# Scores of both head groups in one run of PE tiles inside the batch loop of a fused attention and two-layer kernel

## The chip, the cores and the metric

The kernel runs on one core of one Trainium2 chip. The metric is the device time of one execution in microseconds (us); the time before is 1316.52 us, the median of three runs (1315.59 to 1317.91).

## What is computed

Batch is 8, heads 8, sequence 576, head size 64; `p` holds 32 packed queries per head. All arithmetic is float32.

```python
def sm_attn(qq, kk, vv):
    s = scale * np.matmul(qq, kk.transpose(0, 1, 3, 2))
    s = s - np.max(s, axis=-1, keepdims=True)
    a = np.exp(s)
    a = a / (np.sum(a, axis=-1, keepdims=True) + 1e-09)
    return np.matmul(a, vv)
p_packed = sm_attn(p, k, v)
out = sm_attn(q, p_packed, p_packed)
x = out.transpose(0, 2, 1, 3).reshape(B * S, H * D)      # 4608 x 512
h = np.maximum(np.maximum(x @ w1, x @ w2), x @ w3)       # 512 -> 768
x = h @ w_out                                            # 768 -> 512
h = x @ w_in                                             # 512 -> 2048
return (h * np.cos(h)) @ w_out2                          # 2048 -> 512
```

## The kernel before, in words

**Numbers.** Large products run in three passes on operands split into a rounded part (hi) and a remainder (lo). ACT copies the hi part, DVE or POOL subtracts to get the lo part. Scores, transposes and the small products of attention stay in plain f32.

**Units.** The eight heads of a batch form two head groups, g = 0 and 1, of four heads; `Unit(b, g)` (L413) holds one. Phase 1 of a unit turns p, k and v into the packed rows: `ld_k`, `ld_v` (loads), `S1` (scores of p against k, through `scores`, L451), `S1m` (row maximum, DVE), `E1` (exponential, ACT), `T1` (transposes), `PV1` (product with v and normalization), `BT` (one more transposition, into `bt`). Phase 2 makes the attention weights of the 576 queries: `ld_q`, `S2` (scores of q against `bt`), `S2t` (DVE transpose out of PSUM), `S2r` (maximum and subtraction), `X2a` (exponential), `X2b` (sum and normalization), `X2t` (transpose back), `X2c` (`ch`, `cl`: hi and lo parts). `scores` issues eight products of 64 rows by 32 columns of the PE array: two row halves (hh) by two heads (pi) make four of the array's eight 64x32 tiles, and two steps cover the 576 columns as 2x288. Each f32 product is two matmul instructions in the trace, so one unit's scores are 16 instructions.

**Folds.** The packed rows are multiplied into w1, w2, w3 beforehand. `fold(b, j, g)` (L677) makes piece j (0 to 4, four blocks of 128 columns each, the last half as wide) of group g for batches b and b+1 at once: eight products on all eight 64x32 tiles (`fold_p`, L637), then per half an ACT copy and a DVE subtraction out of PSUM into one of five `zx` buffers, then two DMAs (`fold_z`, L665): one into a z buffer (six of them) for the even batch, one to DRAM for the odd batch.

**Batches.** `gemm1_p` (L707) is one of 18 products h of a batch (12 matmuls each; product u uses fold piece u // 4); `gemm2_p` (L735) are eight half products x after them. A batch has 26 positions: 0 to 17 for h, 18 to 25 for x.

**Stages and their order.** (1) The first stage does the weight conversion and batches 0 and 1. Its order is worked out by a list planner (`Order`, L46) from assumed costs, with random nudges to its priorities given by the list `FIRST`. (2) The loop (L1359) does batches 2 to 5. At position p of batch b, `att_pos` (L853) issues the folds that `FOLDS` places there and the attention steps that `PLANS` places there, before the product of that position; phase 1 works for batch b+2, phase 2 for b+1. `conv_pos` (L820) does the same for pieces of the later weights: load, four passes over ACT, POOL and DVE, store to DRAM. There are NC2 = 18 of these pieces. (3) The last stage does batches 6 and 7, the remaining folds of batch 6, the conversion of the 14 weight pieces that the loop did not do (L1486 to L1508, POOL, ACT, DVE), and the first 16 chunks of the cosine layer (products L1281 and L1388); its order comes from the planner with the list `LAST`. (4) The rest of the cosine layer, in an order of its own (`Flow`).

**PSUM.** `big` (two banks, L421) is the one tile of the attention steps in the loop; `f` is two tiles of one bank each for the folds; `ps_m` holds two tiles for h and x. Every engine works its instructions in the order of issue, and all loads and stores here go through the queue of SP.

Of the kernel before, what the change touches and what calls it, by code (L numbers as in the profile page):

```python
# [29 lines left out]
)  # L30
LAST = (
# [213 lines left out]
def tile_pack_attention_max_moe_cos_moe(  # L245
# [35 lines left out]
    NZX, NCV, NZP, NC2, TS = 5, 6, 6, 18, 2  # L281
# [74 lines left out]
    with tc.manual_schedule():  # L356
# [6 lines left out]
        def small(ap):  # L363
            for _ in range(2):
                ap.tile([P, 4], F32, tag="st", bufs=2, name="st")
            ap.tile([P, 48], F32, tag="ms", name="ms")

        class Res:
            def __init__(self):
# [4 lines left out]
                small(ap)  # L374

        class Res32:
            def __init__(self, n, ps):
# [3 lines left out]
                small(self.ap)  # L381
# [11 lines left out]
        ps_f = mctx.enter_context(tc.tile_pool(name="ps_f", bufs=2, space=PSUM, reuse_waits="tile"))  # L393
# [19 lines left out]
        class Unit:  # L413
# [120 lines left out]
            def Pb(self):  # L534
                self.bd = self.res.ap.tile([P, D], F32, tag="pv", bufs=2, name="pv")
# [35 lines left out]
            def r2(self):  # L571
                ms = self.res.ap.tile([P, 48], F32, tag="ms", name="ms")
# [51 lines left out]

        def w_mov(j, kc):
# [24 lines left out]
        def fold_a(b, j, g, pi):  # L650
            ps = fx[b, j, g][pi]
            x = zx.tile([P, 2, UB * P], F32R, tag="w", name="zx")[:, :, :ps.shape[-1]]
            own = half_of(b, j, pi)
# [3 lines left out]
        def half_of(b, j, pi):  # L657
            return slice(D - pi * D, P - pi * D) if b == 0 and j in alone else slice(0, P)
# [1279 lines left out]
```

## Time and profile before

| What | Value |
|---|---|
| median of three runs | 1316.52 us |
| the profiled execution, its own time | 1318.48 us |
| span of its trace, first to last instruction | 1316.5 us |
| PE (TensorE matmuls) busy | 1274.5 us (97%) |
| DVE (VectorE) busy | 867.5 us (66%) |
| ACT (ScalarE) busy | 684.0 us (52%) |
| POOL (GpSimd) busy | 310.2 us (24%) |
| mean granted clock of TensorE | 0.987 of full speed |

The stages lie in the trace at 0 to 187 us (first), 187 to 449 (loop, some 64 us a batch), 449 to about 730 (last stage) and from there to the end. PE's busy share says that it seldom waits; what a change is worth is read from the waits of its own stage. The profiled execution is 2.0 us above the median of the runs.

### The profile page before, as it was taken

The numbers are of one execution on the slowest core, as the hardware profiler recorded it, in microseconds if no ns is written. First come the engines' busy times: TensorE is split into PE (matmuls) and PEld (weight loads), VectorE is DVE, ScalarE is ACT, GpSimd is POOL, SyncE is SP. The second block draws the span as 40 slices with busy tenths as digits, with TensorE's granted clock in tenths as the row PEclk, the third lists the DMA queues.
The fourth block names the chain that finished last, engine by engine and source line by source line (L and its number), as shares of the span: only waits on it lengthen the run. The fifth ranks groups of instructions, "written<-read, shape, count | busy, mean of one in ns | idle before, by whom it ended". The sixth has DMA issues, their size and how long they took to land.

```text
span 1316.5 us, 24190 instructions
## 1 busy us (share of the span) xinstructions
PE 1274.5 (97%) x9290; PEld 1105.9 (84%) x9290; DVE 867.5 (66%) x1438; ACT 684.0 (52%) x1318; POOL 310.2 (24%) x284
## 2 busy tenths in 40 slices
PE   6789999999999999999999999999999999999998
PEld 3468987988798799977888899999999999999897
DVE  6966455756566662698588696657666576666655
ACT  4543234333323332354455677666666666666665
POOL 4551003351424100261011023212132121321100
PEclk9789999999999999999999999999999999999999
DMA  9877469759975898446012555756557565575630
GB/s 338 290 218 225 141 176 282 275 219 286 288 272 205 247 285 298 177 131 246 33 64 98 182 192 192 237 191 228 185 170 253 186 233 183 170 252 189 219 132 32
DMA packets 111026, 270.54 MB, mean 206 GB/s; under 512 B 15680, under 2 KB 39232, under 8 KB 110912
## 3 DMA queue, kind: packets, MB, share of 16 engines
q1 hardware_dynamic: 110912, 269.01, 61.1%
q8 instruction: 73, 1.20, 0.4%
q14 instruction: 41, 0.34, 0.1%
HBM read 190.32 MB, written 61.87 MB: 192 GB/s over the span
## 4 chain that ended last, share of the span: by engine, by line
PE 87%; DMA 6%; DVE 4%; issue 1%; ACT 1%; SPq 0%; POOL 0%; DVEq 0%; ACTq 0%; POOLq 0%
PE po L1753 27%; PE g L1715 20%; PE h L714 16%; PE x L747 12%; PE g L1281 5%; PE zps L645 2%; PE po L1388 2%; PE big L458 2%; DMA z<-zx 2%; DMA raw<-kT 1%; DMA raw<-v 1%; PE big L526 1%; DMA zd<-zx 1%; DVE y L1308 1%; DMA wraw<-w_out 1%
## 5 line engine op out<-in xcount | busy, mean ns | idle before, releaser
L1753 PE MATMUL po<-w,gh 128*128 128x512 f32 x1560 | 367.5, 390 | 0.0
L1753 PEld LDWEIGHTS po<-w,gh 128*128 128x128 f32 x1560 | 288.1, 188 | 56.5
L1715 PEld LDWEIGHTS g<-xc,wr 128*128 128x128 f32 x2160 | 259.0, 188 | 5.6 <-DVE hs L1738 0.7
L1715 PE MATMUL g<-xc,wr 128*128 128x256 f32 x2160 | 261.8, 278 | 0.2
L714 PE MATMUL h<-at,z 128*128 128x256 f32 (+1 forms) x1728 | 251.5, 302 | 5.4 <-DMA z<-zx 4.6
L714 PEld LDWEIGHTS h<-at,z 128*128 128x128 f32 x1728 | 233.4, 192 | 27.6 <-issue 16.0
L1234 POOL TENSOR_TENSOR xc<-xr,xc 128x256 fp32r<-128x256 f32 x92 | 81.5, 904 | 494.3 <-ACT xc L1230 463.9
L747 PEld LDWEIGHTS x<-hh,w 128*128 128x128 f32 x1152 | 153.8, 190 | 11.8 <-issue 6.2
L747 PE MATMUL x<-hh,w 128*128 128x320 f32 (+1 forms) x1152 | 159.0, 297 | 1.7 <-DVE m L729 1.7
L1738 DVE TENSOR_TENSOR hs<-mc,g 128x256 f32<-128x256 f32 x168 | 70.4, 421 | 136.5 <-PE g L1715 130.0
L729 DVE TENSOR_TENSOR m<-m,h 128x576 f32<-128x576 f32 x96 | 72.2, 752 | 93.3 <-PE h L714 83.6
L1320 ACT ACTIVATE y<-y 128x512 f32<-128x512 f32 x144 | 91.0, 632 | 63.1 <-DVE y L1316 61.6
L1310 DVE SCALAR_TENSOR_TENSOR y<-y 128x512 f32<-128x512 f32 x128 | 96.6, 755 | 41.1 <-ACT y L1302 39.7
L1344 DVE TENSOR_TENSOR gh<-y,gh 128x512 fp32r<-128x512 f32 x144 | 107.8, 749 | 21.9 <-ACT gh L1340 21.0
L1726 ACT COPY mc<-g 128x256 f32<-128x256 f32 x168 | 62.2, 373 | 108.5 <-PE g L1715 108.3
L1340 ACT CAST gh<-y 128x512 fp32r<-128x512 f32 x144 | 89.6, 622 | 49.1 <-DVE y L1324 49.1
L1281 PE MATMUL g<-x,w 128*128 128x512 f32 x384 | 92.0, 389 | 0.0
L1281 PEld LDWEIGHTS g<-x,w 128*128 128x128 f32 x384 | 72.0, 188 | 14.9
L1302 ACT ACTIVATE y<-y 128x512 f32<-128x512 f32 x128 | 81.0, 633 | 4.1
L1324 DVE TENSOR_TENSOR y<-y,hs 128x512 f32<-128x512 f32 x112 | 80.9, 726 | 3.3 <-ACT y L1320 3.1
L1316 DVE TENSOR_SCALAR y<-y 128x512 f32<-128x512 f32 x144 | 78.4, 544 | 3.2
L663 DVE TENSOR_TENSOR zx<-zps,zx 128x512 fp32r<-128x512 f32 (+2 forms) x80 | 48.0, 631 | 36.5 <-ACT zx L654 35.0
(105 smaller groups left out, 1296.4 us busy)
## 6 DMA issues: line engine op xcount, KB each, us to landing
wr<-sd SPq DMA_DIRECT2D x152, 512.0 KB, 4.6
zd<-zx SPq DMA_DIRECT2D x64, 256.0 KB, 4.6
z<-zd SPq DMA_DIRECT2D x32, 512.0 KB, 5.9
z<-zx SPq DMA_DIRECT2D x56, 256.0 KB, 4.6
wr<-sd SPq DMA_DIRECT2D x56, 256.0 KB, 3.6
sd<-w SPq DMA_DIRECT2D x24, 512.0 KB, 4.9
wraw<-w_out SPq DMA_DIRECT2D x22, 512.0 KB, 6.1
wraw<-w SPq DMA_DIRECT2D x18, 512.0 KB, 5.9
```

The lines of the kernel that those rows point to most:

```text
L714: nc.tensor.matmul(ps[:, T0 + c0:T0 + c0 + nt], zt[b, j, g][:, x, c:c + P], at[b, g][:, y, c0:c0 + nt], start=(n == 0), stop=(n == 3 * NG ...
L747: nc.tensor.matmul(ps[:, T0 + c0:T0 + c0 + nt], w[:, x, d * P:(d + 1) * P], hh[f][:, y, c0:c0 + nt], start=(f == 0 and (x, y) == passes[0] ...
L1234: EITHER[eng].tensor_tensor(out=x[:, 1, kk, :], in0=x_part(t, *XSRC[i], kk), in1=x[:, 0, kk, :].bitcast(F32), op=ALU.subtract)
L1281: nc.tensor.matmul(ps, w[:, a, kc * P:(kc + 1) * P], x2[t, kc][:, b, :], start=(n == 0), stop=(n == 3 * KC - 1),)
L1302: nc.scalar.activation(out=r, in_=y, func=AF.Copy, scale=1.0, bias=MAGIC)
L1310: nc.vector.scalar_tensor_tensor(out=y, in0=r, scalar=MAGIC, in1=y, op0=ALU.subtract, op1=ALU.subtract)
L1320: nc.scalar.activation(out=r, in_=y, func=AF.Sin, scale=TWO_PI if c < NF2 else -TWO_PI)
L1324: nc.vector.tensor_tensor(out=r, in0=r, in1=ps, op=ALU.mult)
L1340: nc.scalar.copy(g[:, 0, :], gs[c])
L1344: nc.vector.tensor_tensor(out=g[:, 1, :], in0=gs.pop(c), in1=g[:, 0, :].bitcast(F32), op=ALU.subtract)
L1715: nc.tensor.matmul(ps, w[:, a, c:c + P], x[:, b, kk, :], start=(i < 3 and n == 0), stop=(n == 5), skip_group_check=True,)
L1753: nc.tensor.matmul(po[t][s], g[:, a, s * P:(s + 1) * P], w[:, b, :], start=(f == 0 and i == 0), stop=(f == NF2 - 1 and i == 2),)
```

## The change

Unit g = 1 puts its products on the other four column groups of each row half (`hh ^ g` in every place that says where a row half stands: `scores`, `Pp`, `Bp`, `fold_p`, `half_of`, `fold_z`, `full_a`, `full_d`). In the loop `S1` and `S2` are called once per batch for both units: `both_scores` interleaves their 16 products. Unit 1's scores go into the folds' PSUM, which becomes one tile of two banks. In the first and last stage scores are still made one unit at a time. The loads of k for both units move to positions 22 and 23 of the batch before, `S1` of both to position 4, `S2` of both to 17; the folds of piece 0 and 1 move to positions 19, 21, 23 and 25 of the odd batches, those of piece 2 to 0 and 2 of the even ones. The loop converts 14 weight pieces in place of 18; the last stage converts the other four too. Batch 6's second fold of piece 1 leaves the last stage. The planner of the first and last stage gets new assumed DMA costs and new lists of nudges; the first stage loads k9 in place of v8.

```diff
@@ class Unit, scores / Pp / Bp
-                            c = (2 * (hh ^ swap) + pi) * PK
+                            c = (2 * (hh ^ swap ^ self.g) + pi) * PK
-                            k = 2 * hh + pi
+                            k = 2 * (hh ^ self.g) + pi
+                    has = slice((hh ^ self.g) * D, (hh ^ self.g) * D + D)
-                    nc.tensor.matmul(ps[own], self.bd, ident[:, own], start=True, stop=True)
+                    nc.tensor.matmul(ps[own], self.bd, ident[:, has], start=True, stop=True)
@@ new
+        def both_scores(us, w, x, swap):
+            ps = [us[0].big(), fps[0].tile([P, 2, 512], F32, tag="f", name="big2")]
+            for step in range(2):
+                for hh in range(2):
+                    hf = step ^ hh
+                    for g, u in enumerate(us):
+                        for pi in range(2):
+                            c = (2 * (hh ^ g ^ swap) + pi) * PK
+                            nc.tensor.matmul(
+                                ps[g][c:c + PK, hf, :HS], w(u)[hh * D:(hh + 1) * D, pi, :],
+                                x(u)[pi][hh * D:(hh + 1) * D, hf * HS:(hf + 1) * HS], start=True, stop=True,
+                            )
+            return [p[:, :, :HS] for p in ps]
+        def pair(what, b):
+            us = units[b]
+            if what == "S1":
+                us[0].s1, us[1].s1 = both_scores(us, lambda u: u.pz, lambda u: u.kr, 0)
+                return
+            us[0].s2, us[1].s2 = both_scores(us, lambda u: u.bt, lambda u: u.qr, b % 2)
@@ pools
-    NZX, NCV, NZP, NC2, TS = 5, 6, 6, 18, 2
+    NZX, NCV, NZP, NC2, TS = 5, 6, 6, 14, 2
-        ps_f = mctx.enter_context(tc.tile_pool(name="ps_f", bufs=2, space=PSUM, reuse_waits="tile"))
+        ps_f = mctx.enter_context(tc.tile_pool(name="ps_f", bufs=1, space=PSUM, reuse_waits="tile"))
@@ fold_p
-            banks = fx[b, j, g] = [fps[0].tile([P, 512], F32, tag="f", name="zps")[:, :nw] for _ in range(2)]
+            both = fps[0].tile([P, 2, 512], F32, tag="f", name="zps")
+            banks = fx[b, j, g] = [both[:, hh, :nw] for hh in range(2)]
-                        c = (2 * (hh ^ n) + pi) * PK
+                        c = (2 * (hh ^ n ^ g) + pi) * PK
@@ places in the loop
-            "0:ld_k": -6, "0:ld_v": -4, "0:S1": 0, "0:S1m": 0, "0:E1": 1, "0:T1": 3, "0:PV1": 5, "0:BT": 7,
-            "1:ld_k": 2, "1:ld_v": 4, "1:S1": 8, "1:S1m": 8, "1:E1": 9, "1:T1": 11, "1:PV1": 13, "1:BT": 15,
-            "0:ld_q": 9, "0:S2": 16, "0:S2t": 16, "0:S2r": 17, "0:X2a": 17, "0:X2b": 18, "0:X2t": 18, "0:X2c": 19,
-            "1:ld_q": 11, "1:S2": 19, "1:S2t": 19, "1:S2r": 20, "1:X2a": 20, "1:X2b": 21, "1:X2t": 22, "1:X2c": 23,
+            "0:ld_k": -4, "0:ld_v": 2, "0:S1": 4, "0:S1m": 4, "0:E1": 4, "0:T1": 7, "0:PV1": 9, "0:BT": 11,
+            "1:ld_k": -3, "1:ld_v": 6, "1:S1m": 4, "1:E1": 5, "1:T1": 12, "1:PV1": 14, "1:BT": 16,
+            "0:ld_q": 8, "0:S2": 17, "0:S2t": 17, "0:S2r": 18, "0:X2a": 19, "0:X2b": 20, "0:X2t": 20, "0:X2c": 22,
+            "1:ld_q": 10, "1:S2t": 17, "1:S2r": 18, "1:X2a": 19, "1:X2b": 22, "1:X2t": 22, "1:X2c": 24,
-        FOLDS = {}
-        for j in range(1, NJ):
-            for g, p in enumerate((UB * j - 5, UB * j - 4)):
-                FOLDS.setdefault(p, []).append((j, g))
-        FOLDS[-2] = FOLDS.pop(-1)
-        for g in range(NG):
-            FOLDS.setdefault(2 * g - 2 * KC, []).append((0, g))
+        FOLDS = (
+            {0: (2, 0), 2: (2, 1), 7: (3, 0), 8: (3, 1), 11: (4, 0), 13: (4, 1)},
+            {19: (0, 0), 21: (0, 1), 23: (1, 0), 25: (1, 1)},
+            {0: (1, 1), 1: (2, 0), 2: (2, 1), 7: (3, 0), 8: (3, 1), 11: (4, 0), 13: (4, 1)},
+        )
-            for b, ps in enumerate(((10, 15, 20, 24), (2, 6, 10, 15), (2, 6, 10, 15, 24), (2, 6, 10, 15, 21)))
+            for b, ps in enumerate(((14, 21, 24), (2, 6, 10, 14), (14, 21, 24), (2, 6, 10, 14)))
-                if c == -8:
+                if c == -9:
-                elif c == -2:
+                elif c == -3:
@@ first and last stage
-        LOADS = "k0 k1 v0 v1 q0 q1 k2 k3 v2 v3 q2 q3 k4 v4 k5 v5 k6 v6 q4 k7 v7 q5 k8 v8".split()
+        LOADS = "k0 k1 v0 v1 q0 q1 k2 k3 v2 v3 q2 q3 k4 v4 k5 v5 k6 v6 q4 k7 v7 q5 k8 k9".split()
+        order.RATE, order.LAND = 0.31, 2.8
         order.run(FIRST)
-        for j in range(1, NJ):
+        for j in range(2, NJ):
             for g in range(NG):
-                if (j, g) != (1, 0):
                     quarters(la, j, g, "f2", [("w", piece(j, 2 * g) // 2)] + mine[g:g + 1])
-        order.RATE = 0.26
+        order.RATE, order.LAND = 0.28, 2.8
         order.run(LAST)
```

The lists `FIRST` and `LAST` have other numbers; the planner's accounts of the pools follow (one slot `f` and `f2` of two banks, `pv` 1, `zp` NZP - 4, unit 1's small tiles doubled).

## Rows read from the trace of the kernel before

In the views of busy time the columns are: stretch in us, its length, then busy us (and instructions) of PE, PEld (weight loads), DVE, ACT and POOL, then the granted clock, the DMA share and GB/s. In the views in order of time: start, us, engine, line, operation, and in brackets the idle time before and who ended it.

**Rows 1.** Busy time by engine: first stage, two loop batches, last stage.

```profile
0.00:187.00 187.00, 158.98 (x1534) 122.02 (x1534) 127.31 (x215) 75.56 (x139) 57.53 (x51) 0.94 0.72 231
...
256.00:320.00 64.00, 64.00 (x609) 55.37 (x608) 37.68 (x65) 22.99 (x43) 19.88 (x17) 1.00 0.77 264
320.00:385.00 65.00, 62.02 (x601) 51.88 (x601) 40.43 (x68) 22.67 (x43) 22.70 (x17) 0.97 0.81 266
...
449.00:546.00 97.00, 93.16 (x724) 85.95 (x724) 50.44 (x76) 33.20 (x56) 9.72 (x6) 0.96 0.82 270
546.00:736.00 190.00, 187.55 (x873) 156.43 (x872) 143.35 (x225) 96.47 (x171) 41.78 (x32) 1.00 0.33 118
```

**Rows 2.** Chain that ended last, batch 4 (start us, us, what).

```profile
329.08 3.37 PE h L714 x24
...
332.45 1.02 PE zps L645 x16
...
342.28 7.07 DMA z<-zx
365.85 17.24 PE x L747 x129
383.09 1.10 PE big L458 x16
```

**Rows 3.** The same chain in the first stage: a fold of one batch alone.

```profile
105.15 0.99 PE zps L645 x8
```

**Rows 4.** PE in order of time, batch 4: product 12.

```profile
349.49 2.19 PE L714 MATMUL h<-at,z 128*128 128x256 f32 x9 [2.98 <-DMA z<-zx]
```

**Rows 5.** Busy time by engine in the 3.4 us after that stop.

```profile
349.90:353.30 3.40, 3.40 (x49) 2.73 (x48) 0.17 (x1) 1.20 (x2) 0.24 (x1) 0.51 1.05 349
```

**Rows 6.** SP's queue in order of time, batch 4.

```profile
339.80 1.17 SPq L825 DMA_DIRECT2D wraw<-w_out  x1
341.06 0.48 SPq L674 DMA_DIRECT2D z<-zx  x1
```

**Rows 7.** DMA issues of the whole loop, median us to landing.

```profile
z<-zx SPq DMA_DIRECT2D x34, 256.0 KB, 4.7
```

**Rows 8.** DMA issues of 320 to 349 us, the same columns.

```profile
z<-zx SPq DMA_DIRECT2D x9, 256.0 KB, 6.0
```

**Rows 9.** Groups of instructions: evictions of the folds, maximum and exponential of scores.

```profile
L663 DVE TENSOR_TENSOR zx<-zps,zx 128x512 fp32r<-128x512 f32 (+2 forms) x80 | 48.0, 631 | 36.5 <-ACT zx L654 35.0 <-DMA zd<-zx 1.2
L654 ACT CAST zx<-zps 128x512 fp32r<-128x512 f32 (+2 forms) x80 | 40.8, 546 | 56.4 <-PE zps L645 29.2 <-issue 15.1 <-DMA zd<-zx 11.9
...
L472 DVE TENSOR_REDUCE st<-big 128x1 f32<-128x576 f32 x16 | 12.0, 751 | 4.4 <-PE big L458 4.4
...
L487 ACT ACTIVATE e<-big,st 128x576 f32<-128x576 f32 x16 | 11.9, 742 | 12.2 <-DVE st L476 11.1 <-DVE st L545 1.1
```

**Rows 10.** Groups of instructions: weight conversion in the last stage.

```profile
L1501 DVE SCALAR_TENSOR_TENSOR wm<-wraw,wm 128x512 uint32<-128x512 uint32 x14 | 12.7, 908 | 0.3
...
L1493 DVE SCALAR_TENSOR_TENSOR wm<-wm,w 128x512 uint32<-128x512 uint32 x14 | 10.7, 764 | 5.3 <-ACT wm L1489 5.3
```

**Rows 11.** Busy time by engine, start of the cosine layer.

```profile
566.00:600.00 34.00, 31.55 (x136) 24.93 (x135) 32.74 (x41) 17.25 (x29) 22.10 (x15) 1.00 0.53 175
```

**Rows 12.** PE in order of time, start of the last stage.

```profile
451.60 1.23 PE L458 MATMUL big<-raw,wt 64*32 64x288 f32 x6 [0.98 <-DMA raw<-qT]
...
456.62 1.06 PE L645 MATMUL zps<-w,wt 64*32 64x512 f32 x8 [0.44 <-DVE zx L663]
458.26 1.09 PE L645 MATMUL zps<-w,wt 64*32 64x512 f32 x8 [0.58 <-DVE zx L663]
```

**Rows 13.** Busy time by engine right after.

```profile
459.20:462.60 3.40, 3.40 (x18) 3.32 (x15) 3.33 (x6) 1.75 (x3) 0.00 (x0) 0.50 0.62 166
```

**Rows 14.** PE in order of time, first stage: its longest later stop.

```profile
42.19 1.33 PE L499 MATMUL big<-ident,e 128*128 128x128 f32 x5 [5.68 <-ACT e L487]
```

**Rows 15.** Busy time by engine at the end of odd batch 3.

```profile
290.00:318.50 28.50, 28.50 (x261) 23.16 (x261) 20.49 (x34) 8.20 (x15) 0.99 (x1) 1.00 0.78 226
```

More of the change, by code (lines that the diff above doesn't have):

```diff
@@ L361, in tile_pack_attention_max_moe_cos_moe, with small @@
         rawp = actx.enter_context(tc.tile_pool(name="rawp", bufs=NRAW, side="right"))
-        def small(ap):
+        def small(ap, n):
             for _ in range(2):
                 ap.tile([P, 4], F32, tag="st", bufs=2, name="st")
-            ap.tile([P, 48], F32, tag="ms", name="ms")
+            for _ in range(n):
+                ap.tile([P, 48], F32, tag="ms", bufs=n, name="ms")
         class Res:
@@ L373, in __init__ @@
                 self.wt = [wtp.tile([P, 8, D], F32, tag="x", name="wt") for _ in range(NWT)]
-                small(ap)
+                small(ap, 2)
         class Res32:
@@ L380, in __init__ @@
                 self.pz = self.ap.tile([P, 2, PK], F32, name="pz")
-                small(self.ap)
+                small(self.ap, 1)
         raw_src = []
@@ L652, in fold_a, with half_of @@
             x = zx.tile([P, 2, UB * P], F32R, tag="w", name="zx")[:, :, :ps.shape[-1]]
-            own = half_of(b, j, pi)
+            own = half_of(b, j, g, pi)
             nc.scalar.copy(x[own, 0, :], ps[own])
             fx[b, j, g, pi] = ps, x
-        def half_of(b, j, pi):
-            return slice(D - pi * D, P - pi * D) if b == 0 and j in alone else slice(0, P)
+        def half_of(b, j, g, pi):
+            return slice((1 ^ pi ^ g) * D, (1 ^ pi ^ g) * D + D) if b == 0 and j in alone else slice(0, P)
         def fold_d(b, j, g, pi):
             ps, x = fx[b, j, g, pi]
-            own = half_of(b, j, pi)
+            own = half_of(b, j, g, pi)
             nc.vector.tensor_tensor(out=x[own, 1, :], in0=ps[own], in1=x[own, 0, :].bitcast(F32), op=ALU.subtract)
@@ L670, in fold_z @@
                 zt[b, j, g] = zp.tile([P, 2, UB * P], F32R, tag="w", name="z")
-            own, oth = slice(pi * D, pi * D + D), slice(D - pi * D, P - pi * D)
+            own, oth = (slice((h ^ pi ^ g) * D, (h ^ pi ^ g) * D + D) for h in range(2))
             if not only:
@@ L691, in full_d @@
             for hh in range(2):
[L692 removed]
+                ps, own = fx[0, j, g][hh], slice((hh ^ g) * D, (hh ^ g) * D + D)
                 nw = ps.shape[-1]
@@ L770, in gemm2 @@
             if hf:
-                gemm2_d(b, d, gemm2_s(b, d))
+                gemm2_d(b, d, gemm2_s(b, d, nc.scalar.copy))
         g2ps = {}
@@ L860, in att_pos @@
             bb = b + b % 2
-            if 2 <= bb < B:
-                for j, g in FOLDS.get(p - NPOS if b % 2 else p, []):
-                    fold(bb, j, g)
+            folds = FOLDS[2 if b == 2 else b % 2]
+            if p in folds:
+                fold(bb, *folds[p])
             for _, who, ahead, what in steps.get(p, []):
                 us = units.get(b + ahead)
-                if us:
+                if us and what in ("S1", "S2"):
+                    pair(what, b + ahead)
+                elif us:
                     getattr(us[who], what)()
@@ L917, in tile_pack_attention_max_moe_cos_moe @@
             prev = item
-        order.hold(raws["k8"] + raws["v8"])
+        order.hold(raws["k8"] + raws["k9"])
         def own(i, name):
@@ L1049, in quarters @@
             who = (1,) if only else (0, 1)
-            banks = [(pool, ("F", b, j, g, pi, "f")) for pi in range(2)]
+            bank = ("F", b, j, g, "f")
             add(
@@ L1053, in quarters @@
                 ([("Ba", 2 * b + 2 * n + g) for n in who] + [("wm", piece(j, 2 * g + pi)) for pi in range(2)]) * (b < B - 2),
-                banks, keep,
+                [(pool, bank)], keep,
             )
@@ L1073, in tile_pack_attention_max_moe_cos_moe @@
                     key = ("A", j, g)
-                    banks = [("f", key + (hh, "f")) for hh in range(2)]
+                    bank = key + ("f",)
                     add(
                         key + ("p",), "PE", 0.95 * w, lambda j=j, g=g: fold_p(0, j, g, (0,)),
-                        [("Ba", g)] + [("wm", piece(j, 2 * g + pi)) for pi in range(2)], banks,
+                        [("Ba", g)] + [("wm", piece(j, 2 * g + pi)) for pi in range(2)], [("f", bank)],
                     )
@@ L1080, in tile_pack_attention_max_moe_cos_moe @@
                         key + ("a",), "ACT", 1.0 * w, lambda j=j, g=g: full_a(j, g), [key + ("p",)],
-                        [("zp", ("Z", 0, j, g))], [t for _, t in banks],
+                        [("zp", ("Z", 0, j, g))], [bank],
                     )
@@ L1084, in tile_pack_attention_max_moe_cos_moe @@
                         key + ("d",), VE, 1.2 * w, lambda j=j, g=g: full_d(j, g), [key + ("a",)], [],
-                        [t for _, t in banks] + [("Z", 0, j, g)],
+                        [bank] + [("Z", 0, j, g)],
                     )
@@ L1414, in tile_pack_attention_max_moe_cos_moe @@
             order.owner["Z", la, 0, g] = "zp"
-        order.owner["Z", la, 1, 0] = "zp"
+            order.owner["Z", la, 1, g] = "zp"
         for n in range(NU // 2):
@@ L1447, in tile_pack_attention_max_moe_cos_moe @@
                 gap = ("H", la, NU - 1) if j < 3 else ("H", lb, UB * j - 9)
-                done = [("F", la, j, g, pi, "z") for pi in range(2)] if (j, g) > (1, 0) else []
+                done = [("F", la, j, g, pi, "z") for pi in range(2)] if j > 1 else []
                 spread(lb, j, g, done + [gap])
```

23 lines of the change are left out of this document (11 added, 12 removed), and 20 rows, old and new, of tables (FIRST, LAST).

## The prediction

> **What bounds the kernel now.** I read the busy time of the engines by stage first, because the 97% of PE is an average over stages with different limits. In the loop, batch 3 has PE busy for all of its 64.0 us at full clock, with DVE at 37.7 and ACT at 23.0; batch 4 is 62.0 of 65 [rows 1]. The loop is PE's: an instruction taken from PE there is time, as long as nothing else ends later. The first stage is not: PE is busy 159.0 of 187 us at a clock of 0.94, and waits for loads, conversions and softmax chains. The last stage has 3.8 us of PE idle in its first 97 and 2.5 in the next 190, where DVE is at 75% [rows 1]. Second I read the chain that ended last, which in the loop is PE itself but for a few links. In batch 4 one head group's scores hold it for 1.10 us, a fold for 1.02, two products h for 3.37 (1.68 each), and once a DMA, 7.07 us long, is the link [rows 2].
>
> **Part A, the scores.** One unit's scores use four of the eight 64x32 tiles in two rounds. The pair puts the other unit on the idle four. The trace has this comparison in the folds: a fold of one batch alone, four tiles, holds the chain for 0.99 us [rows 3], a fold of two batches, eight tiles and twice the instructions, for 1.02 [rows 2]. So the second four tiles cost 0.03 us a round, 0.06 for two: a pair takes 1.10 + 0.06 = 1.16 us in place of 2 x 1.10 = 2.20, 1.04 less. The loop makes S1 for batches 4 to 7 and S2 for 3 to 6, eight pairs: **-8.3 us**. Bounds: the tiles hide fully (1.10, -8.8), or they don't overlap at all (0, a rival below). I take the folds' value, since they are f32 on the same tiles and lack only the second round.
>
> One rule speaks against it. The Trainium skill, "TensorE: Matmul & The Clock Gate", Part 3, says that a weight load runs beside a matmul in flight only when their row group differs; in a pair four column groups of one row half follow one another, so by it the pair would take about two units' time and part A would be 0. The folds, which have that order too, don't show such a cost.
>
> **Part B, the stop in batch 4.** Product 12, the first to need fold (3, 1), stops for 2.98 us until 349.49 [rows 4]; the clock is at half in the 3.4 us that follow (0.51, all of it busy), which costs 1.7 [rows 5]: 4.7 together. The z transfer was late at SP: its issue at 341.06 stood behind a weight-piece load of 1.17 us [rows 6], and landing took 6.0 us there against 4.7 over the loop [rows 7, 8]. After the change the even batches have four pieces fewer to convert between them, fold (1, 1) has left batch 4, and so have k and a store or two from positions 0 to 13. But the cover shrinks too: S1 of unit 1 stood between fold (3, 1) and product 12 and leaves. From the fold's end PE has four products (6.7 us) and a half-wide fold, a product with v and a small transposition, which I estimate at 1.7 from a whole fold's 1.02 [rows 2]; the transfer needs two copies and two subtractions, each but the first copy beside another (0.55 + 2 x 0.63, some 1.9 with the steps between) [rows 9], SP's issues (three at 0.48 or more, about 1.6) and 4.7: equal within a few tenths. I take **-3.3**, a stop of some 0.7 in each of the two even batches left over, between -4.7 (gone) and +4.7 (this price in both).
>
> **Part C, four more conversions in the last stage.** Each adds 0.76 + 0.91 us on DVE [rows 10], 6.7 for four, with ACT and POOL beside. In the stretch where they would run DVE is busy 32.7 of 34 us and PE idle for 2.5 [rows 11]. After it DVE has a quarter free [rows 1], and most pieces are needed one chunk of products after another, not at once. So most is put off rather than lost: **+1.0**, between 0 and +8.4 (all 6.7 and a fall to half clock of 1.7, as in rows 5).
>
> **Part D, the start of the last stage.** PE stops 0.98 us for q and 0.44 and 0.58 for the folds' PSUM [rows 12], then has 3.4 us at half clock [rows 13]: 3.7 in all. One fold of seven leaves this place, and its transfers with it; the order is new, so I count less than half: **-1.5**, between -3.7 and +2.0 (the same stops once more).
>
> **Part E, the new order of the first stage.** Its counts hardly change (a load of k for one of v). What moves is the order, which no row shows. The nearest row is its longest stop after the first loads, 5.68 us on an exponential [rows 14]. **0**, between -6 (it is filled) and +6 (one more like it).
>
> **Part F, new waits in the loop.** The pair's second half sits in the folds' PSUM. At position 4 two maxima and two exponentials follow S1: 2 x 0.75 on DVE, then 0.74 twice on ACT, the first beside the second maximum [rows 9], some 3 us, and the next fold comes after three products, 5.0 us. At position 17 two DVE transposes must end before fold (0, 0) at 19, two products later. A fold at 2 has two products (3.4) for its four evictions before S1 wants the bank; only batch 2 has three folds in a row, for some 0.3 us of stop each. The chains end later and closer: the tail of an odd batch, with all of phase 2 in it, has DVE busy 20.5 of 28.5 us [rows 15], and fold (1, 1) adds two subtractions there, 1.3 [rows 9]: it still fits, and `cl` of unit 1 goes out at 24, two half products (18 matmuls each, 2 x 18 / 129 of 17.24 us, 4.8) ahead of its reader [rows 2]. If this cover fails, the product at position 0 is late by what DVE lags. The loads of k stand 8 positions ahead of S1, past the z loads and x2 stores on SP, for landings of some 6 us. **+0.6**, between 0 and +5.
>
> One-bank against two-bank folds cost nothing: the two halves that waited apart [rows 12] end at the same time as one whole fold that waits for both. Column groups exchanged for g = 1 change no count, and the last part, `Flow`, is untouched.
>
> **Sum:** -8.3 - 3.3 + 1.0 - 1.5 + 0 + 0.6 = -11.5. The profiled execution took 1318.5 (span 1316.5), 2.0 above the median of 1316.5: it becomes 1307.0, the median **1305.0 us**.
>
> **The rivals.**
> - *The shared bank stops PE (slower).* If E1 of unit 1 or its S2t is late, the fold behind it waits on PE, and all products behind that. The places are fold (3, 0) at position 7 of the even batches and fold (0, 0) at 19 of the odd ones, four in all. Price: the wait for an exponential in the first stage, 5.68 us [rows 14], four times 22.7; with -11.5 that is +11.2, 1328. It decides from 2.9 us a place. For it: ACT and DVE work in order, and a late zx buffer holds both. Against it: 5.0 us of cover for some 3.
> - *Tiles beyond four don't overlap.* The second unit's 16 instructions follow the first's on the same row halves, as two separate scores do now, 2 x 1.10 [rows 2]: part A is 0 and the time 1313.3. For it: a pair has four PSUM banks and two rounds, a fold two banks and one. Against it: the folds [rows 2, 3]. This is where the rule named in part A would lead.
> - *The last stage gives it back.* Part C is 8.4: 1312.4. For it: DVE is at 96% where the pieces land [rows 11]. Against it: the slack behind.
> - *The stop at product 12 stays, in both even batches.* Part B is +4.7: 1313.0. For it: the cover shrinks by one unit's scores. Against it: less traffic on SP and DMA.
> - *The new orders fill the first stage's stops.* Part E is -6: 1299.0.
>
> **The numbers.** The forecast has 0.55; the slower rival 0.05, no overlap 0.08, the last stage 0.12, the stop 0.10, the filled first stage 0.10. A measurement of this kernel tells about 0.2% (2.6 us) from no change. Faster by more: 0.55 and 0.10, half of no overlap (0.04), 0.09 of the last stage and 0.07 of the stop, 0.85. Within: 0.03 + 0.02 + 0.02 = 0.07. Slower: 0.05 and 0.01 from each of the three, 0.08. The range runs from 1297 (the filled first stage with part D gone too) to 1313 (the three rivals at the edge).
>
> **What would show it.** A pair at 1.1 to 1.3 us with 32 instructions in the PE's order of time, where 2.20 stood; two pairs a batch; batches of the loop at about 62 us; PE still busy throughout. Part B: no wait of product 12 above 1 us and no half clock in the loop. Part C: PE's stops at the start of the cosine layer no larger than 2.5 us in sum. Part F: no wait of zps or big on an exponential or a DVE transpose. The forecast is wrong if the pair takes over 2 us, if a fold or a pair waits over a microsecond in each batch, or if the first or last stage is longer by more than 8 us.

## The result and the profile after

The changed kernel takes 1302.7 us, the median of four runs (1302.05 to 1305.66); the kernel before took 1316.8 beside it (1315.59 to 1317.91). The ratio is 0.9906, with a 95% interval of 0.989 to 0.9923: 14.1 us less. The forecast was 1305.0 with a range of 1297 to 1313, so the direction and the size were right; the terms that make up the size were not all right, as the stages show.

I cut both traces at the same three pieces of work: the first fold of batch 2, the first fold of the last stage, and the first product of `Flow`. The view is busy time by stage; its columns are those of [rows 1]. The kernel before:

```profile
0.00:190.08 190.08, 162.06 (x1554) 124.91 (x1554) 128.36 (x216) 76.23 (x140) 57.53 (x51) 0.94 0.72 231
190.08:443.36 253.28, 249.74 (x2409) 212.99 (x2408) 155.22 (x263) 92.00 (x173) 84.97 (x63) 0.99 0.78 257
443.36:729.51 286.15, 279.85 (x1609) 240.18 (x1609) 195.47 (x303) 129.80 (x226) 51.50 (x38) 0.99 0.51 176
729.51:1316.50 586.99, 582.88 (x3721) 527.85 (x3719) 388.49 (x656) 385.93 (x780) 116.17 (x132) 1.00 0.56 190
```

The changed kernel:

```profile
0.00:185.99 185.99, 154.26 (x1554) 120.46 (x1555) 127.95 (x216) 76.33 (x141) 57.86 (x49) 0.95 0.74 239
185.99:431.65 245.66, 240.82 (x2425) 209.40 (x2424) 142.45 (x242) 97.67 (x182) 70.06 (x56) 1.00 0.78 250
431.65:713.54 281.89, 275.50 (x1593) 237.82 (x1593) 199.52 (x309) 134.27 (x234) 61.67 (x44) 0.99 0.51 175
713.54:1300.80 587.26, 582.89 (x3721) 527.84 (x3719) 388.83 (x656) 385.63 (x780) 115.74 (x132) 1.00 0.55 189
```

The reader is to see four differences: the first stage is 4.1 us shorter, the loop 7.6, the last stage 4.3, and the flow 0.3 longer, 15.7 together on spans of 1316.5 and 1300.8 (the medians differ by less: the profiled execution of before, 1318.48, was 1.7 above the median given here, and this one, 1302.58, is 0.1 below). The counts of PE say that one fold (16 instructions, 1.02 us [rows 2]) has moved from the last stage into the loop (2409 to 2425, 1609 to 1593). On equal work the loop is therefore 8.6 us shorter and the last stage 3.2. DVE loses 12.8 us of the loop and gains 4.1 in the last stage. The conversions that moved are the smaller part of the 12.8: the section on the change leaves out that `gemm2` in the loop now copies x out of PSUM with `nc.scalar.copy`, so that these copies move from DVE (15 between the cuts, 11.3 us) to ACT (16, 10.2 us). One of them in order of time, before and changed:

```profile
254.30 0.76 DVE L757 COPY x2s<-x 128x576 f32<-128x576 f32 x1 [1.87 <-PE x L747]
```

```profile
431.76 0.64 ACT L787 COPY x2s<-x 128x576 f32<-128x576 f32 x1 [1.65 <-PE x L777]
```

No run takes this one line back, so what it is worth is not shown.

PE in order of time shows what the loop saved. Two pairs, one of `S1` and one of `S2`, the first with the work that follows it:

```profile
197.95 1.20 PE L641 MATMUL big<-raw,pz 64*32 64x288 f32 x32
199.08 5.00 PE L744 MATMUL h<-at,z 128*128 128x256 f32 x36
...
229.28 1.20 PE L641 MATMUL big<-raw,wt 64*32 64x288 f32 x32
```

32 instructions hold PE for 1.13 us, from 197.95 to 199.08, where 2 x 1.10 stood [rows 2] (the length in a line runs to the end of the last instruction, which overlaps what follows). All eight pairs show the 1.20.

The same view gives every stop of PE above a quarter of a microsecond in the loop (the brackets: us of idle time, and who ended it):

```profile
189.77 1.09 PE L675 MATMUL zps<-w,wt 64*32 64x512 f32 x16 [0.91 <-DVE zx L693]
193.55 1.09 PE L675 MATMUL zps<-w,wt 64*32 64x512 f32 x16 [0.90 <-DVE zx L693]
...
207.79 1.09 PE L675 MATMUL zps<-w,wt 64*32 64x512 f32 x16 [0.43 <-DVE zx L693]
227.88 1.48 PE L744 MATMUL h<-at,z 128*128 128x256 f32 x9 [0.93 <-DMA z<-zx]
...
325.07 1.09 PE L675 MATMUL zps<-w,wt 64*32 64x512 f32 x16
...
328.85 1.09 PE L675 MATMUL zps<-w,wt 64*32 64x512 f32 x16 [0.43 <-DVE zx L693]
329.87 1.84 PE L744 MATMUL h<-at,z 128*128 128x256 f32 x12
...
340.68 1.50 PE L744 MATMUL h<-at,z 128*128 128x256 f32 x9 [1.24 <-DMA z<-zx]
```

Waits for the folds' PSUM are 2.67 us in all, waits for z 2.17. The 2.98 us stop of [rows 4] and the half clock of [rows 5] are gone; the loop's clock is 1.00.

In the last stage the same view has one large stop, and smaller ones at the folds and in the cosine layer:

```profile
448.32 1.96 PE L675 MATMUL zps<-w,wt 64*32 64x512 f32 x16 [3.44 <-DVE zx L693]
...
457.50 0.67 PE L675 MATMUL zps<-w,wt 64*32 64x256 f32 x16 [0.77 <-DVE zx L693]
...
579.60 2.56 PE L1419 MATMUL po<-w,gh 128*128 128x512 f32 x10 [0.93 <-DVE gh L1375]
...
602.34 2.56 PE L1419 MATMUL po<-w,gh 128*128 128x512 f32 x10 [0.69 <-DVE gh L1375]
```

Who ended the 3.44 us is a chain of two. DVE had waited for ACT; ACT's copy into a `zx` buffer had waited for that buffer's transfer to DRAM, and on SP four loads of q stood ahead of these transfers. DVE in order of time, then ACT, then SP:

```profile
446.88 1.29 DVE L693 TENSOR_TENSOR zx<-zps,zx 128x512 fp32r<-128x512 f32 x2 [6.55 <-ACT zx L684]
```

```profile
446.27 0.58 ACT L684 CAST zx<-zps 128x512 fp32r<-128x512 f32 x1 [4.02 <-DMA zd<-zx]
```

```profile
435.89 1.88 SPq L455 DMA_DIRECT2D raw<-qT  x4
```

### The profile page after: what moved, and what is told of

Read it like the earlier page. It is cut to its first block, busy times and chain, and to the rows that moved or that the text cites. A ratio compares the mean times of both kernels' runs of the same rounds, so it can differ in the third digit from the quotient of the medians.

```text
span 1300.8 us, 24232 instructions
## 1 busy us (share of the span) xinstructions
PE 1253.5 (96%) x9290; PEld 1095.5 (84%) x9290; DVE 858.8 (66%) x1423; ACT 693.9 (53%) x1336; POOL 305.3 (23%) x281
## 4 chain that ended last, share of the span: by engine, by line
PE 59%; DVE 4%; ACT 1%; issue 1%; DVEq 0%; ACTq 0%
PE po L1783 27%; PE g L1745 21%; PE g L1312 5%; PE x L777 3%; PE h L744 3%; PE po L1419 1%; DVE y L1339 1%; DVE wm L1531 1%; DVE gh L1375 0%; DVE y L1347 0%; DVE y L1331 0%; DVE wm L1523 0%; ACT w L1537 0%; ACT y L1324 0%; DVE y L1355 0%
## 5 line engine op out<-in xcount | busy, mean ns | idle before, releaser
L744 PEld LDWEIGHTS h<-at,z 128*128 128x128 f32 x1728 | 230.5, 190 | 31.3 <-issue 14.0
```

The lines of the kernel that those rows point to most:

```text
L744: nc.tensor.matmul(ps[:, T0 + c0:T0 + c0 + nt], zt[b, j, g][:, x, c:c + P], at[b, g][:, y, c0:c0 + nt], start=(n == 0), stop=(n == 3 * NG ...
```

## The experiments

Every edit is to the changed kernel, and each ratio is to the kernel before on the same chip. "Loop" and "last stage" are the lengths between the three cuts above. A distance from the changed kernel is one of medians that need not be from the same chip; where it is large, the one by the ratios (times 1316.8 us) stands beside it.

**1. Without the exchange of column groups.** Everything stays as in the changed kernel, the paired calls too, but both units use the same column groups.

```diff
-                            c = (2 * (hh ^ g ^ swap) + pi) * PK
+                            c = (2 * (hh ^ swap) + pi) * PK
...
-                            k = 2 * (hh ^ self.g) + pi
+                            k = 2 * (hh) + pi
```

(and so in the other places that name a row half)

> The changed kernel with the column exchange of g = 1 taken out everywhere; both units' scores are still issued as one pair, at the same places, with the same instructions and PSUM, but they now share four tiles. Theory (the gain is the idle four tiles): a pair takes twice one unit's 1.10 us on PE in place of the 1.13 it takes now, 8 x 1.07 = 8.6 us more than the changed kernel, some 1311.3, with all other terms as they are. Rival (the gain comes from one call in place of two, and from the new places): the pair stays near 1.2 us and the time within 1.5 us of 1302.7.

Measured: 1311.62 us (1308.48 to 1315.33), ratio 0.9967 (0.995 to 0.9985): 8.9 above the changed kernel, 8.0 by the ratios. Its pair in PE's order of time, and its loop as busy time:

```profile
201.33 2.17 PE L641 MATMUL big<-raw,pz 64*32 64x288 f32 x32
```

```profile
189.39:442.73 253.34, 248.78 (x2426) 213.66 (x2425) 142.49 (x242) 97.74 (x182) 70.03 (x56) 1.00 0.75 242
```

The pair takes 2.17 us, twice one unit, and the loop is 7.7 us longer than the changed kernel's 245.66, eight pairs at 0.97. Calling the units together gains next to nothing by itself (2.17 against 2 x 1.10); the idle tiles are what pays. The rival that tiles beyond four don't overlap falls. The rule on which it leaned (the Trainium skill, "TensorE: Matmul & The Clock Gate", Part 3: a weight load runs beside a matmul in flight only if the row groups differ) doesn't tell 1.20 from 2.17 us here: both have the same order of row halves, and only the column groups differ. The measurement decides.

**2. One unit's products after the other's.** The order of issue, which interleaved the two units, is undone; the tiles stay exchanged.

```diff
-            for step in range(2):
-                for hh in range(2):
-                    hf = step ^ hh
-                    for g, u in enumerate(us):
+            for g, u in enumerate(us):
+                for step in range(2):
+                    for hh in range(2):
+                        hf = step ^ hh
```

> The changed kernel with the columns exchanged, but the 16 products of unit 0 issued ahead of the 16 of unit 1 in place of interleaved. Theory (PE issues in order and a product waits only for its own tile): unit 1's first round runs beside unit 0's second, three rounds in place of two, some 1.6 us a pair; 8 x 0.5 = 4 us more than the changed kernel, 1306.7. Rival one (the order of issue does not matter, the tiles have queues of their own): no change, 1302.7. Rival two (only what is issued side by side overlaps): 2.2 us a pair, 1311.

Measured: 1302.38 us (1300.8 to 1306.24), ratio 0.99 (0.9877 to 0.9924), no difference from the changed kernel. The pairs in PE's order of time:

```profile
199.52 1.41 PE L641 MATMUL big<-raw,pz 64*32 64x288 f32 x32
...
229.91 1.23 PE L641 MATMUL big<-raw,wt 64*32 64x288 f32 x32
```

They take 1.23 to 1.41 in place of 1.20. The interleaving gives 0.03 to 0.21 us a pair, 0.7 over all eight, too little to see in the times; three rounds of work one after another, my theory for this order, fall.

**3. The order of the first stage as before.** The old list `FIRST` and the old planner costs come back for the first stage alone.

```diff
-        order.RATE, order.LAND = 0.31, 2.8
```

> The changed kernel with the first stage's list of nudges and assumed DMA costs of before. In the trace the loop starts 4.1 us earlier after the change. Theory (that is the new order alone): the loop starts at 190 us again and the time is some 4 us up, 1306.7; loop and last stage keep their lengths. Rival (it comes from the new material: k9 in place of v8, one bank pair for folds): the loop starts at 186 and the time stays within 1 us.

Measured: 1306.92 us (1302.83 to 1308.83), ratio 0.9926 (0.9905 to 0.9947), 4.2 above the changed kernel, 2.6 by the ratios, and the intervals overlap. The cut at the first fold of batch 2 lies at 190.31, as before (190.08). In PE's order of time the stop of [rows 14] is 6.04 us there and 5.22 in the changed kernel, which is a small part of the difference. First this kernel, then the changed one:

```profile
42.96 1.33 PE L503 MATMUL big<-ident,e 128*128 128x128 f32 x5 [6.04 <-ACT e L491]
```

```profile
40.57 1.33 PE L506 MATMUL big<-ident,e 128*128 128x128 f32 x5 [5.22 <-ACT e L494]
```

The new order brings the first stage's gain, but less than the 4.1 us of the two profiles. The twelve profiles in this study that have the new order put the cut at 185.99 to 189.39 us, 187.9 on the mean, the two that have the old one at 190.08 and 190.31; so some 2.3 us are the order's, and the changed kernel's own profile was an early one. This run's profile, its slowest execution, has a longer loop as well, 246.96 us with 3.03 us of waits for z.

**4. The order of the last stage as before.** The old list `LAST` and the old cost, on the new material (one fold fewer, four conversions more).

```diff
-        order.RATE, order.LAND = 0.28, 2.8
+        order.RATE = 0.26
```

> The changed kernel with the last stage's list of nudges and assumed DMA costs of before. In the trace the last stage (from its first fold to the first product of the last part) takes 281.9 us after the change and 286.2 before, of which one fold, 1.0, went into the loop. Theory (the rest is the new order): 285 us, the time 3 us up, 1305.7. Rival (the rest is one fold's transfers less at its start): 282 us, no change. Second rival (four more conversions cost nothing only because the new order places them well): PE stops at the start of the cosine layer, 5 us or more up.

Measured: 1308.32 us (1305.62 to 1311.92), ratio 0.9943 (0.9923 to 0.9964), 5.6 above the changed kernel, 4.9 by the ratios; its last stage is 288.82 us in place of 281.89. Its largest stops, in PE's order of time:

```profile
442.38 1.08 PE L462 MATMUL big<-raw,wt 64*32 64x288 f32 x2 [2.33 <-DMA raw<-qT]
...
527.34 11.24 PE L774 MATMUL x<-hh,w 128*128 128x256 f32 x72 [1.73 <-DVE m L756]
...
556.43 3.03 PE L1309 MATMUL g<-x,w 128*128 128x512 f32 x12 [2.87 <-ACT x2s L784]
```

q, the maximum of batch 7 and a copy of x ahead of the cosine layer are late. So the lighter start alone does not make the last stage shorter: with the old nudges it is 2.7 us longer than before (286.15) though it has a fold less. The new list is 6.9 us better there in these traces, and part of that pays for the four conversions. This is not the old order, though: the planner gives its nudges to the operations by their place in the list, and on another list of operations the old numbers fall on other ones. So the 6.9 us compare a list chosen for this material with one that wasn't.

**5. Folds of pieces 3 and 4 a position earlier**, to take away the waits for z at products 12 and 16.

```diff
-{0: (2, 0), 2: (2, 1), 7: (3, 0), 8: (3, 1), 11: (4, 0), 13: (4, 1)}
+{0: (2, 0), 2: (2, 1), 6: (3, 0), 7: (3, 1), 11: (4, 0), 12: (4, 1)}
```

> The changed kernel with the folds of piece 3 one position earlier (6 and 7) and the second of piece 4 too (12), so that their transfers have one product, 1.68 us, more before products 12 and 16. In the changed kernel these products still wait 0.93 and 1.24 us for z. Theory (the stops are the transfer's length against the cover): both go, 2.2 us less in the profile, about 1301. Rival (the transfer is not the limit, SP's queue or the buffers are): the stops stay, or the fold at 6 waits for the exponential that holds its PSUM, and the time is the same or higher.

Measured: 1304.0 us (1301.61 to 1305.25), ratio 0.9907 (0.9883 to 0.9932): no gain. No wait for z is left in its loop. What stands in their place, in PE's order of time (the same in batch 4):

```profile
209.01 1.09 PE L675 MATMUL zps<-w,wt 64*32 64x512 f32 x16 [1.14 <-DVE zx L693]
```

The second fold of piece 3 now waits 1.14 us for the PSUM of the first, where it waited 0.43, in both even batches: the transposition that stood between the two folds (0.52 us from 205.03 to 205.55 in the changed kernel) now follows them. The loop takes 244.76 us, 0.9 below the changed kernel's 245.66, within what loops of equal kernels differ by (below).

**6. k loaded four positions earlier**, at 18 and 19 of the batch before.

```diff
-            "0:ld_k": -4,
+            "0:ld_k": -8,
...
-            "1:ld_k": -3,
+            "1:ld_k": -7,
```

> The changed kernel with the loads of k four positions earlier in the loop (18 and 19 in place of 22 and 23). Theory (their place costs nothing as long as they land before position 4): no change, 1302.7 within 2 us, no wait of the scores on k in either. Rival (late loads were needed to keep SP and the DMA engines free for the folds and stores at the end of a batch): x2 stores, z loads or folds are late and PE stops in the odd batches, 2 us or more.

Measured: 1302.26 us (1301.29 to 1304.03), ratio 0.9897 (0.987 to 0.9923), loop 244.52. No difference: late loading of k neither costs nor brings time where it stands.

**7. q of batch 7 behind the third fold of the last stage**, to free the stop of 3.44 us.

```diff
-            add(f"q{i}", "SP", 1.1, uu[i].ld_q, [], [("raw", t) for t in raws[f"q{i}"]], data=0.6)
+            add(f"q{i}", "SP", 1.1, uu[i].ld_q, [("F", la, 3, 0, 1, "z")], [("raw", t) for t in raws[f"q{i}"]], data=0.6)
```

> The changed kernel with the loads of q for batch 7, in the last stage, held back behind the first fold of piece 3; nothing else in the planner's input changes, and the nudges fall on the same operations. In the changed kernel a fold at the start of the last stage stops PE for 3.44 us, since ACT waits for a zx buffer whose DMA is still under way behind these loads, and the clock is at half for the 6.8 us around it. Theory: without the loads in front the buffer is free in time, the stop and most of the half clock go, 3 to 6 us less, about 1298. Rival (five zx buffers turn over too slowly whatever else is under way): the stop stays and the time is the same. Second rival (batch 7's attention comes late in turn): a new stop between batch 6 and 7.

Measured: 1307.66 us (1305.06 to 1310.5), ratio 0.9935 (0.9912 to 0.9958), 5.0 above the changed kernel, 3.8 by the ratios; the intervals just overlap. PE in order of time:

```profile
454.75 0.67 PE L675 MATMUL zps<-w,wt 64*32 64x256 f32 x16 [2.32 <-DVE zx L693]
...
457.78 2.94 PE L465 MATMUL big<-raw,wt 64*32 64x288 f32 x16 [2.37 <-DMA raw<-qT]
```

The stop at the fourth whole fold is gone, so the q loads did set it off at this place. But two others, 4.69 us together, have come, one for the zx buffers at the second half-wide fold and one for q itself. The last stage is 284.47 us, 2.6 longer.

**8. Experiments 5 and 7 together.**

> The earlier folds and the later q loads together. If both theories hold the gains add up, some 5 to 8 us under the changed kernel, about 1296; if only one of them holds, its own gain; nothing in the one touches the other's place.

Measured: 1306.61 us (1302.76 to 1309.06), ratio 0.9926 (0.9902 to 0.995). The last stage is 282.40, q's stop 1.40 + 0.86 in place of 2.37. Neither gain is in the time, as neither was in experiments 5 and 7.

**9. q behind the second fold.** As experiment 7, with `("F", la, 2, 1, 1, "z")`.

> The four loads of q for batch 7 are held until the second fold's z transfer of the last stage is issued (in the changed kernel they stand ahead of the first one, in the run that held them behind the third fold they came too late). Theory (the transfers of the folds lose their place on SP to 1.9 us of q issues, and the five zx buffers come free late): the 3.44 us stop at the fold falls under 1.5 us without the stop of 2.4 us for q that came with the later place: last stage some 279 to 280 us in place of 281.9, time about 1300.5. Rival (the stretch has more transfers than buffers, so the stop only changes its name): the stops of the first 30 us of the last stage still sum to 4 us or more, and the time stays at 1302 to 1304 or grows.

Measured: 1301.83 us (1298.92 to 1304.92), ratio 0.9889 (0.9859 to 0.9919). The stop of 3.44 us has become one of 2.38, at the second half-wide fold; q no longer waits:

```profile
452.99 1.11 PE L675 MATMUL zps<-w,wt 64*32 64x256 f32 x16 [2.38 <-DVE zx L693]
```

The last stage is 280.06 us. So the second half of the theory held (q is in time) and the first didn't (2.38 against 1.5); the time can't be told from the changed kernel's.

**10. Half of q behind the second fold**: only the second head group's two loads wait for it.

> Only the two loads of q for the second head group are held behind the second fold, those of the first head group stay ahead of all folds. Theory: half of the 1.9 us of issues leaves the folds' way, and the stop of 3.44 us falls to some 2.5 us without any wait for q: time about 1301.5. Rival: the stop moves to the next fold or to the scores of the second head group, sum of stops as in the changed kernel (4.5 us in the first 30 us of the last stage): 1302 to 1304.

Measured: 1300.37 us (1297.82 to 1303.5), ratio 0.9878 (0.9849 to 0.9907). The folds' largest stop, in PE's order of time:

```profile
450.76 0.67 PE L675 MATMUL zps<-w,wt 64*32 64x256 f32 x16 [0.76 <-DVE zx L693]
```

The large stop is gone and none of its size has come; the last stage is 278.28 us, the shortest of all. Since its interval overlaps the changed kernel's, the two were run once more side by side.

**11 and 12. The kernel of experiment 10 and the changed kernel again, on one chip.**

> The kernel with half of the q loads behind the second fold once more, beside the changed kernel on the same chip, since the trace has its last stage 3.6 us shorter (278.3 against 281.9 us) and the earlier intervals overlap. If the gain of the last stage is real: about 1299.5, 2 to 4 us under the changed kernel of the same call. Rival (the first stage's own spread of some 3 us between executions covers it): medians within 1.5 us of each other.

> The changed kernel as it is, beside the run above on the same chip: 1302.5, last stage 281 to 282 us from its first fold to the first product of the flow, with the 3 us stop at the fourth whole fold of it. Rival: this stop was an accident of one execution, and the last stage is some 279 us here.

Measured: 1302.42 us (1297.82 to 1304.98), ratio 0.9896 (0.9875 to 0.9917), and 1303.43 us (1301.64 to 1305.26), ratio 0.9906 (0.9887 to 0.9926). They differ by 1.0 us, and the intervals overlap widely. The last stages are 280.60 and 280.03: in this profile of the first kernel the half-wide fold waits 1.99 us where it waited 0.76 above. The gain of experiment 10 is not shown; no version of this study is measurably faster than the changed kernel. The large stop of the changed kernel is no accident: it is 3.37 us here, though the last stage is 1.9 us shorter than in its first profile (the clock, in the last section, is part of it).

```profile
450.81 1.09 PE L675 MATMUL zps<-w,wt 64*32 64x512 f32 x16 [3.37 <-DVE zx L693]
```

## Why the prediction was right, and where its terms were not

**Part A held.** The pair takes 1.13 us where 1.16 was foreseen; eight of them save 8 x (2.20 - 1.13) = 8.6 us against 8.3. The folds were the right row to price it by, and experiment 1 shows the cause: it takes away only the exchange and loses 8.0 to 8.9 us, most of the 14.1. A small term was left out: four folds of the loop before stood directly ahead of a unit's scores, which began 0.88 us after them and not 1.02; that overlap, 0.6 us in all, is gone.

**Part B was about right.** Waits for z of 0.93 and 1.24 us, without half clock, stand where 0.7 in each even batch was foreseen. The prediction counted 4.7 us before and left out a shorter wait for z in batch 2, in PE's order of time:

```profile
222.08 1.48 PE L714 MATMUL h<-at,z 128*128 128x256 f32 x9 [0.56 <-DMA z<-zx]
```

With it 5.2 became 2.2, a gain of 3.1 against 3.3. It is the term that varies. Eight profiles have this loop unchanged; they take 243.7 to 247.0 us, and mostly follow their waits for z: 243.7 with 0.5 us of them (experiment 10), 243.9 with 0.7 (4), 244.4 with 0.9 (11), 244.4 with 1.0 (9), 245.1 with 1.5 (12), 245.7 with 2.2 (the profile above), 246.7 with 2.9 (7) and 247.0 with 3.0 (3). The stop is thus something that runs from a half to three microseconds, and that the forecast met 3.3 is partly luck.

**Part F was too small**, and three sentences of the prediction failed with it. "Only batch 2 has three folds in a row, for some 0.3 us of stop each": the stops are 0.91 and 0.90. "One-bank against two-bank folds cost nothing": they do. And part B's "each but the first copy beside another" no longer holds. In the kernel before, DVE starts to subtract the first half beside ACT's copy of the second; in the changed kernel it waits for both copies. ACT and DVE in order of time, before and changed:

```profile
198.50 1.07 ACT L654 CAST zx<-zps 128x512 fp32r<-128x512 f32 x2
199.11 1.29 DVE L663 TENSOR_TENSOR zx<-zps,zx 128x512 fp32r<-128x512 f32 x2 [1.23 <-ACT zx L654]
```

```profile
326.31 1.07 ACT L684 CAST zx<-zps 128x512 fp32r<-128x512 f32 x2 [0.50 <-PE zps L675]
327.41 1.29 DVE L693 TENSOR_TENSOR zx<-zps,zx 128x512 fp32r<-128x512 f32 x2 [3.05 <-ACT zx L684]
```

That is 0.61 us from the first copy's start to the subtraction, and 1.10; in each of the 20 folds of the loop before DVE starts before the second copy has ended, in none of the 21 of the changed loop. So with one tile the whole of both copies and both subtractions, 3.78 us from the first fold's start (325.07 to 328.85, and 185.99 to 189.77), stands ahead of the next fold, and the subtraction that the z transfer needs comes 0.49 us later behind its copy too. An estimate from these rows: with the 0.49 us back, the four stops of 2.67 us would be 0.83. No run tried it.

The kernel before has the same sequence twice, a fold, a transposition, a product and the next fold. In batch 2 PE goes on almost without a pause; in batch 4 the second fold has a pause inside it:

```profile
197.03 1.09 PE L645 MATMUL zps<-w,wt 64*32 64x512 f32 x16
...
200.31 1.21 PE L645 MATMUL zps<-w,wt 64*32 64x512 f32 x16
201.45 1.85 PE L714 MATMUL h<-at,z 128*128 128x256 f32 x12
...
321.50 1.09 PE L645 MATMUL zps<-w,wt 64*32 64x512 f32 x16
...
324.81 1.66 PE L645 MATMUL zps<-w,wt 64*32 64x512 f32 x16
326.40 1.85 PE L714 MATMUL h<-at,z 128*128 128x256 f32 x12
```

From the first fold's start to the work after the second is 4.42 and 4.90 us there and 4.80 in the changed kernel (325.07 to 329.87, above). With two tiles the second fold can begin before the first is read out whole (at 324.81, while DVE reads until 325.35), but in batch 4 that gained nothing over one tile. Such pauses inside folds are 0.7 us in the loop before (0.12 and 0.57 here), the waits for the folds' PSUM 2.7 in the changed one: +2.0 in place of +0.6. The chains that share this PSUM with the second unit's scores cost nothing: no fold or pair waits for an exponential or a DVE transpose, so the slower rival had no ground. Loading k late, the last point of this part, cost nothing either (experiment 6). DVE, which this part feared for at the end of odd batches, was also relieved of the x copies, which the prediction didn't count.

**The loop in sum:** -8.0 - 3.1 + 2.0 = -9.1 by these measured terms, with the 0.6 us taken off part A, and -8.6 by the cuts on equal work; -11.0 was foreseen.

**Part D failed.** It gave -1.5 on the ground that one fold of seven leaves the start of the last stage. That was the wrong thing to count: what ends last there is the five zx buffers and the SP queue that empties them. Take the start as the time to the first half product x of batch 6, and the rest as what lies behind it. PE in order of time, the first half product of batch 6 and that of batch 7, before and changed:

```profile
486.81 19.20 PE L747 MATMUL x<-hh,w 128*128 128x256 f32 x144
...
536.30 8.68 PE L747 MATMUL x<-hh,w 128*128 128x256 f32 x54 [1.74 <-DVE m L729]
```

```profile
476.28 19.02 PE L777 MATMUL x<-hh,w 128*128 128x256 f32 x144 [0.25 <-DVE m L759]
...
523.63 9.64 PE L777 MATMUL x<-hh,w 128*128 128x256 f32 x72
```

The start is 43.4 us before and 44.6 in the changed kernel, with a fold less in it: +2.2 on equal work, just beyond the bound of +2.0. With four whole folds in a row, and q's loads between them, it has stops of 3.44 + 0.77 + 0.31 + 0.25 and 2.6 us of half clock (5.28 us of busy PE at 0.50):

```profile
446.80:453.60 6.80, 5.28 (x30) 3.65 (x31) 4.75 (x7) 2.47 (x6) 1.43 (x1) 0.50 0.71 192
```

That is 7.4 us in place of 3.7; the start grew by less because the start of before lost time inside its groups too (a fold in two halves of 8 instructions, over a microsecond each [rows 12]). And it varies: in the six profiles with this stage unchanged (the changed kernel's two and experiments 2, 3, 5 and 6) the start is 42.3 to 44.8 us, -0.1 to +2.3 on equal work, +1.1 on the mean. Experiments 7 to 10 show the q loads as what sets the large stop off at this fold. DVE's wait for both copies is in this chain as well: the first half was copied at 441.66 and subtracted only at 446.88, when the second copy had got its buffer. Which of the two is worth more is not shown.

**Part C was too large, and something outside it gave more back.** Behind the start the last stage is 5.4 us shorter (242.7 to 237.3). The four conversions cost PE nothing to be seen: its stops on `gh` in the cosine layer are 0.93 + 0.69, where the kernel before had 2.5 us of PE idle [rows 11]. And a stop that the prediction hadn't priced is gone: before, the first half product x of batch 7 waited 1.74 us for a maximum and then had 1.7 us of half clock; the changed order has no wait there (the lines above). Experiment 4 has this stop again, at 1.73 us, so it hangs on the planner's list. These two make 3.4 and 0.8 of the 5.4; the other 1.2 us lie in PE's busy time, not in stops, and I can't place them line by line. In sum the last stage is 3.2 us shorter on equal work in the profile and 5.1 in its repetition (286.15 - 280.03 - 1.02), where parts C and D together gave 0.5.

**Part E was too cautious.** 0 was taken for lack of a row; -4.1 was in the profile, and about -2.3 belongs to the order (experiment 3). In the profile the rival of the filled stops (-6) was nearer than the main case, on the mean it wasn't, and the stop it named is still there.

In sum, the two profiles lie 4.1 us further apart than forecast: the first and last stage gave 4.1 and 2.7 us more than the terms E and C with D, the loop 2.4 less than A, B and F, and the flow is 0.3 longer. The medians lie only 2.3 us from the forecast, since the profiled execution of before was one of its slower ones. The mechanism of the largest term is shown; that the rest came out so near is in part luck, since D, E, F and the unpriced maximum missed in both directions.

## What to carry to other kernels

Price idle tiles of the PE array by a neighbour in the same trace that uses them: a fold on four tiles and on eight told the saving of a pair to within 0.03 us. When an order is planned anew, don't price a stage by the share of work that leaves it; ask which buffers and which queue end last there, and what now stands ahead of them on that queue. A stop moved by one position came back here as a wait for the buffer next in the chain (experiments 5 and 7), so read the whole stage's length and not the stop alone. And when two tiles become one, look at who reads which half: here a reader of the first half came to wait for the reader of the second.

## What the runs showed of the hardware that I had not expected

The order of issue hardly matters for the overlap of tiles here: the 16 instructions of one unit and then the 16 of the other take 1.23 to 1.41 us, interleaved 1.20, and on shared tiles 2.17.

The same stop isn't always followed by a lower clock. In the changed kernel's first profile PE idles 3.44 us before the fold at 448.32 and is granted half the clock (1.2 GHz) for the 6.8 us from 446.8 on; in its second it idles 3.37 us before the fold at 450.81, after the same work, and the clock stays at 1.00 (2.4 GHz). Experiment 2 idles only 2.31 us before that fold and is at 0.50 from 448.5 to 451.5. Busy time by engine of the second profile, 6.8 us around the stop, to be held against the line under part D:

```profile
449.50:456.30 6.80, 5.42 (x66) 4.16 (x70) 5.38 (x8) 2.77 (x6) 1.42 (x1) 1.00 0.74 201
```

And a stage that waits for its first loads wasn't equally long each time: in the twelve profiles the same order of the first stage ended anywhere from 185.99 to 189.39 us.
